# Windowed attention and an ELU feed-forward on one core: first q and k blocks on SyncE, small first tiles, stores on ScalarE

## The chip, the core and the metric

The kernel runs on one core of one Trainium2 chip. The core has five engines that run side by side and meet only at semaphores: TensorE (PE in the profile; its weight loads are listed as PEld), VectorE (DVE), ScalarE (ACT), GpSimd (POOL) and SyncE (SP). SyncE computes nothing here; it asks for transfers. ScalarE and GpSimd can ask for transfers too. Each engine works through its own instructions in the order in which the program gives them, so an instruction that waits holds up everything behind it on its engine. Transfers run on 16 DMA engines; those asked for by GpSimd can change float32 to bfloat16 on the way, those asked for by SyncE or ScalarE cannot.

The metric is the device time of one execution in microseconds, as a median over several runs. The traces are single profiled executions.

## What is computed

```python
# q, k, v: (8, 8, 576, 64) float32; w_in: (512, 2048); w_out: (2048, 512)
scores = (q @ k.transpose(0, 1, 3, 2)) / sqrt(64)
scores = where(abs(pos[:, None] - pos[None, :]) <= 32, scores, -1e9)
attn = softmax(scores)                                # over keys
x = (attn @ v).transpose(0, 2, 1, 3).reshape(4608, 512)
h = x @ w_in
g = where(h > 0, h, exp(min(h, 0)) - 1)
out = g @ w_out                                       # (4608, 512) float32
```

## The kernel before, in words

**Units, groups, tiles.** A unit is 64 query rows of one batch for all 8 heads; nine units make a batch, 72 make the problem. Attention runs over groups of two units (`G`, lines 333 to 337; 37 entries, some of one unit). The feed-forward runs over tiles of units, `sizes = [4, 5, 4, 3] + [8] * 7` (line 494), so that a full tile has 512 token columns.

**One group of attention.** `QK` (line 345) multiplies transposed keys by transposed queries, `SM` (line 355) takes the exponential on ScalarE, `MK` (line 368) multiplies by the window mask on VectorE, `AV` (line 380) multiplies by the values, with a column of ones that gives the sum, `RN` (lines 394 and 396) divides on VectorE, and `X` turns the result for the feed-forward: for the first `NC0 = 8` groups by TensorE and a ScalarE copy (lines 412 and 418), after that by a transposing DMA that SyncE asks for (line 408). The turned columns of a tile lie in `xt`, of which there are two buffers.

**One tile of the feed-forward.** For each of 16 slices `fo` of the 2048 columns, `H` (line 436) runs four matmuls into a PSUM bank `psH` (three banks), `EX` (line 445) takes the exponential on ScalarE, `FF` makes min(e - 1, 0) up to sign, on ScalarE (line 455) or on VectorE (line 457) as `fact` says, and `GG` (lines 463 and 466) takes the maximum on VectorE into `g_sb`. `pack` joins two slices where a tile has four units. `Y` (line 481) multiplies a chunk of 128 tokens by `w_out`, 16 matmuls; `YC` (line 487) copies the bank on ScalarE; `OUT` (line 491) stores 256 KB to DRAM, asked for by SyncE.

**Inputs.** The weights go by eight GpSimd requests that cast (`WI` line 514, `WO` line 519). q and k of batches 0 and 1 go by GpSimd requests too (`LR`, line 307), half a batch per tensor in two requests; TensorE turns them in small transposes (`TR`, line 319), and `ER` copies them out. Those of batch 0 lie in parts of `g_sb` meanwhile, those of batch 1 in the third buffers of `vw` and `qT`. All v blocks, and q and k of batches 2 to 7, are loaded as float32 by SyncE (`L`, line 241) into `st` buffers (14); GpSimd casts them (line 256; batch 0 on VectorE and ScalarE), and for q and k SyncE then asks for a transposing DMA (`XB`, line 273). `GT` (line 249) writes one element of an `st` buffer, so that the load behind it starts no earlier.

**What sets the order.** `Plan` holds every operation with engine, duration, rank, what it depends on, and what it takes and gives back. `Plan.run` plays them through in a small model of engines and DMA rings, on each engine the ready one of lowest rank first, and then issues them in that order. The model's durations, its counts of `st`, `cb`, `psH` and of ring places so decide the written order on each engine's queue; on the chip that order is fixed and only the semaphores decide when each starts. GpSimd's requests have a list of their own (`LINE`, line 579), with at most eight open at a time ("swq").

```python
    LINE = [("0kA",), ("0qA",), ("id",), ("mask",), ("WI", 0), ("WI", 1),
            ("0kB",), ("0qB",), ("WI", 2), ("WI", 3), ("WO", 0), ("WO", 1),
            ("WO", 2), ("1kA",), ("1qA",), ("WO", 3), ("1kB",), ("1qB",)]
```

A transposing DMA of q or k of batch 2 also waits until every `TR` of batch 1 is done, since those read from the buffers that it writes (lines 635 to 640).

Of the kernel before, what the change touches and what calls it, by code (L numbers as in the profile page):

```python
# [20 lines left out]
class Plan:  # L21
# [29 lines left out]
    def run(self):  # L51
# [40 lines left out]
        while len(order) < len(ops) or events or any(rings.values()):  # L92
            heads = [q[0] for q in rings.values() if q]
            per = len(heads)
# [49 lines left out]
            if dma is not None:  # L144
                ring, pk, ns = dma
                heapq.heappush(events, (now + self.QLAT[ring], 2, (
                    ring, [n, pk * ns / 1000.0])))
# [12 lines left out]
def kernel(  # L160
# [33 lines left out]
    NTA = 3  # L194
    NC0 = 8
    NST = 14
# [10 lines left out]
    xtp = ctx.enter_context(tc.tile_pool(name="xtp", bufs=2))  # L207
# [22 lines left out]
    def rows(nm, j):  # L230
        if nm != "v":
            return 128 * j, min(128, S - 128 * j), 0
# [3 lines left out]
    def L(b, nm, j, eng):  # L236
        lo, n, r = rows(nm, j)
# [13 lines left out]

    def copy(eng, dst, src):
# [5 lines left out]
    def C(b, nm, j, eng):  # L258
        _, n, _ = rows(nm, j)
# [5 lines left out]
    def dstT(b, nm, j):  # L265
        _, n, _ = rows(nm, j)
# [4 lines left out]
    def XB(b, nm, j):  # L271
        _, n, _ = rows(nm, j)
        nc.sync.dma_start_transpose(dstT(b, nm, j), live.pop(("C", b, nm, j))[0:n])

# [153 lines left out]
    def pack(t):  # L428
        return 2 if tiles[t][1] == 4 else 1
# [18 lines left out]
    def fact(t, fo):  # L448
        return fo // pack(t) % 2 == 1 if t < NTA else True
# [40 lines left out]
    def OUT(c):  # L490
        nc.sync.dma_start(out[c * 128:c * 128 + 128, :], ys.pop(c))

    NCH = N_TOK // 128
    sizes = [4, 5, 4, 3] + [8] * 7
    tiles, where, tof = [], {}, {}
    p0 = 0
    for t, n in enumerate(sizes):
        for u in range(p0, p0 + n):
            tof[u] = t
            if u == G[gof[u]][0]:  # L500
# [6 lines left out]
              "cb": NCB, "swq": 8, "ring": 2.5})  # L507
# [17 lines left out]
    PER = 4.0  # L525
    LEAD = 36.0
# [47 lines left out]
    def group_of(b, nm, j):  # L574
        if nm == "q":
# [3 lines left out]
    LINE = [("0kA",), ("0qA",), ("id",), ("mask",), ("WI", 0), ("WI", 1),  # L579
            ("0kB",), ("0qB",), ("WI", 2), ("WI", 3), ("WO", 0), ("WO", 1),  # L580
            ("WO", 2), ("1kA",), ("1qA",), ("WO", 3), ("1kB",), ("1qB",)]
    rk = -2000.0
    for x in LINE:
        rk += 1
        if x[0] in ("WI", "WO"):
            fn = {"WI": WI, "WO": WO}[x[0]]
            P.op(x, "POOL", 0.75, rk, [], lambda fn=fn, c=x[1]: fn(c),
                 dma=("P", 32, 104), acq=("swq", 1), rel=("swq", 1))
# [4 lines left out]
        else:  # L593
            b, nm, half = int(x[0][0]), x[0][1], "AB".index(x[0][2])
            for two in range(2):
                P.op(("LR", b, nm, half, two), "POOL", 0.6, rk + 0.1 * two, [],
                     lambda b=b, nm=nm, half=half, two=two: LR(b, nm, half, two),
                     dma=("P", 12, 80), acq=("swq", 1), rel=("swq", 1))
    PK = {"q": [64] * 4 + [32], "k": [64] * 4 + [32], "v": [48] + [64] * 3 + [48]}
    for b in range(B):  # L600
        blocks = sorted(((group_of(b, nm, j), "kqv".index(nm), nm, j)
                         for nm in "kqv" for j in range(NTB)))
        for _, _, nm, j in blocks:
            if b < NBR and nm != "v":
# [3 lines left out]
            eng, ring = "SP", "S"  # L608
            deps = [[], [("GT", b, nm, j)], [("LR", 1, "k", 1, 0)]][min(b, 2)]
            if b == 1:  # L610
                P.op(("GT", b, nm, j), "DVE", 0.1, r - 60, [("WO", 0)],
                     lambda b=b, nm=nm, j=j: GT(b, nm, j))
            P.op(n, eng, 0.4, r - (30 if b > 1 else 60 if b else 1000), deps,
                 lambda b=b, nm=nm, j=j, eng=eng: L(b, nm, j, engs[eng]),
                 dma=(ring, PK[nm][j], 18 if b < 2 else 19), acq=[("st", 1), ("ring", 1)])
            if nm == "v":
                for part in range(3):
# [6 lines left out]
                    if b == 0:  # L624
                        eng = "ACT" if j == 2 or part == 2 and j > 2 else "DVE"
                    P.op(("CV", b, j, part), eng, {"DVE": 0.45, "POOL": 0.7, "ACT": 0.6}[eng],
                         r - 8 + 0.1 * part, deps,
# [3 lines left out]
            P.op(("C", b, nm, j), "POOL", 0.72, r - 8, [n],  # L631
                 lambda b=b, nm=nm, j=j: C(b, nm, j, nc.gpsimd),
                 acq=("cb", 1), rel=("st", 1))
            war = [("QK", last(b - NKB))] if b >= NKB else []
# [3 lines left out]
            P.op(("TT", b, nm, j), "SP", 1.2, r - 6, [("C", b, nm, j)] + war,  # L638
                 lambda b=b, nm=nm, j=j: XB(b, nm, j),
                 dma=("S", 32, 19), acq=("ring", 0.5), rel=("cb", 1))  # L640
    for b in range(NBR):
        for half in range(2):
            r = prank(gof[b * NQB + 4 * half])
            for nm in "kq":
                for part in range(2):
# [6 lines left out]
                    P.op(("TTR", b, nm, half, part), eng, 0.75, r - 4,  # L652
# [152 lines left out]
```

## Time and profile before

| | |
|---|---|
| median of 13 runs | 347.31 us (344.74 to 350.44) |
| the profiled execution | 348.27 us, of it the span from first to last instruction 346.0 us |
| mean granted TensorE clock | 0.98 |
| read from and written to DRAM | 36.70 MB, 9.44 MB |
| requests on SyncE's queue | 100 loads, 60 transposes of q and k, 29 of x, 36 stores |

A profiled span is divided into the busy time of each engine. Requests for transfers are listed apart, as SPq, POOLq and ACTq, with the time for which the engine was held by them; that is not the time of the transfer. In a view of windows each row is one stretch of the span: its length, the busy time of each engine with its number of instructions, the granted TensorE clock, the DMA share (summed over queues, so that it can pass 1) and the bytes moved per time. In a timeline each row has start, duration, engine, line, operation and, in brackets, how long the engine was idle before and what ended that. In a view of one line the durations are least, median and most in nanoseconds, followed by the first and last start.

### The profile page before, as it was taken

How to read it: one execution, taken by the hardware profiler on the slowest of the kernel's cores; microseconds unless marked ns; L12 is line 12 of the kernel's file. 1: busy time of each engine (PE TensorE's matmuls, PEld its weight loads, DVE VectorE, ACT ScalarE, POOL GpSimd, SP SyncE). 2: the span in 40 equal slices, each digit the busy share in tenths (PEclk: the TensorE clock that was granted, in tenths of full speed). 3: DMA queues.
4: the chain of work that ended last, by engine and by line, in shares of the span. 5: the costliest groups of instructions: out<-in, count | busy, mean ns of one | idle time of the engine just before them, and what ended most of it. 6: DMA issues, size and time to landing. Idle time of an engine off the chain costs nothing.

```text
span 346.0 us, 7586 instructions
## 1 busy us (share of the span) xinstructions
PE 308.0 (89%) x2848; PEld 165.0 (48%) x2848; DVE 190.0 (55%) x434; ACT 233.8 (68%) x400; POOL 116.0 (34%) x193
## 2 busy tenths in 40 slices
PE   1598889989989978996999989985999999999995
PEld 1476556666654434442445444432454454444442
DVE  7447878885466576663266646551555655443400
ACT  1748675856778776985478768762778788777711
POOL 8341195755245455344425442436100000000000
PEclk9999999999999999999799999996999999999999
DMA  9999994999998989899899879999431111210021
GB/s 162 204 206 205 205 173 81 231 159 203 206 196 154 234 161 181 152 232 153 189 171 217 182 170 157 209 167 229 86 99 47 45 47 45 68 40 30 33 91 61
DMA packets 151620, 50.89 MB, mean 147 GB/s; under 512 B 139808, under 2 KB 146976, under 8 KB 151584
## 3 DMA queue, kind: packets, MB, share of 16 engines
q1 hardware_dynamic: 144032, 43.86, 66.3%
q0 software_dynamic: 7552, 6.56, 12.0%
q8 instruction: 22, 0.36, 0.4%
q14 instruction: 14, 0.11, 0.1%
HBM read 36.70 MB, written 9.44 MB: 133 GB/s over the span
## 4 chain that ended last, share of the span: by engine, by line
PE 62%; DMA 23%; POOL 3%; DVE 3%; SPq 3%; ACT 3%; issue 2%; POOLq 0%; DVEq 0%; ACTq 0%
PE psH L436 27%; PE psY L481 15%; PE psT L481 11%; DMA qT<-cb 8%; DMA vw<-in_q_dram 4%; DMA xt<-xs 4%; PE psO L380 3%; DMA w_in_sb<-in_moe_w_in_dram 3%; PE psS L345 2%; DMA kT<-cb 2%; SPq L241 2%; DMA st<-in_k_dram 1%; ACT pu L355 1%; DMA st<-in_v_dram 1%; PE psS L481 1%
## 5 line engine op out<-in xcount | busy, mean ns | idle before, releaser
L436 PE MATMUL psH<-xt,w_in_sb 128*128 128x512 bf16 (+3 forms) x704 | 154.3, 349 | 13.1 <-DMA xt<-xs 10.3
L445 ACT ACTIVATE e<-psH 128x512 f32<-128x512 f32 (+2 forms) x160 | 88.3, 555 | 69.9 <-PE psH L436 67.4
L463 DVE SCALAR_TENSOR_TENSOR g_sb<-f,psH 128x512 bf16<-128x512 bf16 (+2 forms) x144 | 91.0, 635 | 50.9 <-ACT f L455 50.4
L436 PEld LDWEIGHTS <-w_in_sb 128*128 128x128 bf16 x704 | 65.3, 100 | 67.0 <-issue 14.3
L455 ACT ACTIVATE f<-e 128x512 bf16<-128x512 f32 (+2 forms) x144 | 85.3, 594 | 3.7
L481 PE MATMUL psY<-w_out_sb,g_sb 128*128 128x512 bf16 x320 | 82.8, 383 | 0.0
L481 PEld LDWEIGHTS <-g_sb 128*128 128x128 bf16 x576 | 53.9, 98 | 58.7 <-issue 2.6
L256 POOL CAST vw<-st 64x512 bf16<-64x512 f32 (+3 forms) x98 | 61.9, 632 | 51.3 <-DMA st<-in_v_dram 45.1
L256 POOL CAST cb<-st 128x512 bf16<-128x512 f32 (+1 forms) x60 | 37.3, 624 | 61.5 <-DMA kT<-cb 33.3
L481 PE MATMUL psT<-w_out_sb,g_sb 128*128 128x512 bf16 x224 | 57.1, 379 | 0.0
L368 DVE TENSOR_TENSOR pm<-pu,masks 128x512 bf16<-128x512 bf16 x72 | 33.5, 505 | 38.3 <-ACT pu L355 38.2
L355 ACT ACTIVATE pu<-psS 128x1024 bf16<-128x1024 f32 (+1 forms) x37 | 37.0, 1000 | 7.8 <-PE psS L345 7.7
L380 PEld LDWEIGHTS <-pm 128*128 128x128 bf16 x576 | 27.5, 100 | 16.6 <-DVE pm L368 2.0
L394 DVE RECIPROCAL rc<-psO 128x4 f32<-128x4 f32 (+1 forms) x71 | 12.8, 180 | 37.5 <-PE psO L380 36.9
L380 PE MATMUL psO<-vw,pm 128*128 128x65 bf16 x552 | 30.1, 196 | 1.9 <-DVE xs L396 0.9
L396 DVE TENSOR_TENSOR xs<-psO,rc 128x256 bf16<-128x256 f32 (+1 forms) x71 | 30.1, 424 | 2.5
L345 PE MATMUL psS<-qT,kT 64*128 64x64 bf16 x576 | 16.2, 193 | 8.2 <-DMA qT<-cb 6.0
L345 PEld LDWEIGHTS <-kT 64*128 64x128 bf16 x576 | 11.7, 96 | 20.8 <-issue 20.4
L319 PE MATMUL psH<-ident,g_sb 48*64 48x48 bf16 x192 | 6.1, 225 | 9.0 <-DMA g_sb<-in_k_dram 7.6
L487 ACT COPY y<-psY 128x512 f32<-128x512 f32 x20 | 11.5, 574 | 3.2 <-PE psY L481 2.9
L319 PEld LDWEIGHTS <-g_sb 48*64 48x64 bf16 x192 | 5.5, 151 | 9.5 <-DMA g_sb<-in_k_dram 7.7
L487 ACT COPY y<-psT 128x512 f32<-128x512 f32 x14 | 8.0, 571 | 2.9 <-PE psT L481 2.9
(48 smaller groups left out, 88.6 us busy)
## 6 DMA issues: line engine op xcount, KB each, us to landing
out_dram<-y SPq DMA_DIRECT2D x36, 256.0 KB, 2.6
st<-in_v_dram SPq DMA_DIRECT2D x24, 256.0 KB, 3.9
st<-in_k_dram SPq DMA_DIRECT2D x24, 256.0 KB, 4.0
st<-in_q_dram SPq DMA_DIRECT2D x24, 256.0 KB, 4.1
st<-in_v_dram SPq DMA_DIRECT2D x16, 192.0 KB, 3.8
w_in_sb<-in_moe_w_in_dram POOLq DMA_DIRECT2D x4, 512.0 KB, 11.8
w_out_sb<-in_moe_w_out_dram POOLq DMA_DIRECT2D x4, 512.0 KB, 13.5
st<-in_k_dram SPq DMA_DIRECT2D x6, 128.0 KB, 3.3
```

What stands on the lines that cost most here:

```text
L256: eng.tensor_copy(dst, src)
L345: nc.tensor.matmul(psS[:, h % 2, s, hp, :], lhsT=kT[b % NKB][base:base + 64, hp, qb * QB:qb * QB + 128], rhs=qT[b % NKB][base:base + 64, h ...
L355: nc.scalar.activation(pu[:, :, 0:n], live.pop(("S", i))[:, :, 0:n], AX.Exp, scale=SCALE)
L368: nc.vector.tensor_mul(dst, pu[:, :, s], mb)
L380: nc.tensor.matmul(o[:, j, :], lhsT=p[:, h, s * QB:s * QB + 128], rhs=vw[b % NVB][:, qb, h, :], start=(s == 0), stop=(s == len(G[i]) - 1))
L396: nc.vector.tensor_mul(live["X", i][0:n, g * HP:(g + 1) * HP, :], o[0:n, :, 0:D], rb)
L436: nc.tensor.matmul(ps[:, f], lhsT=w_in_sb[:, do, (fo + f) * 128:(fo + f + 1) * 128], rhs=xts[t][:, do, :], start=(do == 0), stop=(do == ND ...
L445: nc.scalar.activation(e, ps, AX.Exp)
L455: nc.scalar.activation(f, e, AX.Relu, bias=1.0, scale=-1.0)
L463: nc.vector.scalar_tensor_tensor(g_sb[:, fo:fo + pack(t), gcols(t)], f, -1.0, ps, ALU.mult, ALU.max)
L481: nc.tensor.matmul(ps, lhsT=g_sb[:, fo, gc:gc + 128], rhs=w_out_sb[:, fo, :], start=(fo == 0), stop=(fo == NFO - 1))
L487: nc.scalar.copy(y, ys.pop(c))
```

## The change

The first half of q and k of batch 0 no longer comes by GpSimd's casting requests. SyncE loads it as float32 blocks of 128, 128 and 32 rows (`rows`), first in its queue and mixed with the v blocks (`FIRST`); VectorE casts the k blocks, ScalarE the q blocks, TensorE turns each in four transposes into a `psH` bank (`T`), and ScalarE (k) or VectorE (q) copies it out (`E`). GpSimd makes the identity and the masks first, and then runs a copy of one element (`WAIT`) that reads the landed block `v 0`; all its requests come behind that.

The feed-forward tiles become `[2, 2, 2, 3, 4, 3] + [8] * 7`, with four, two and two slices joined in tiles of 2, 3 and 4 units. `xt` has three buffers instead of two, `st` 12 instead of 14. Nine groups instead of eight are turned by TensorE. In tiles 0 to 4 `FF` alternates between ScalarE and VectorE as it did in tiles 0 to 2; in the tiles of eight units every fourth `FF` goes to VectorE where all were on ScalarE. Stores are asked for by ScalarE, behind the copy `YC`. For batches 2 to 7 the ranks of loads, casts and transposes are 36, 18 and 14 ahead where they were 30, 8 and 6. `H` operations of the first six tiles are no longer tied to one another in order, and the model's durations, ring places and sharing between rings are changed, all of which can alter the written order.

```diff
-    NTA = 3
-    NC0 = 8
-    NST = 14
+    NTA = 5
+    NC0 = 9
+    NXT = 3
+    NST = 12
...
-    xtp = ctx.enter_context(tc.tile_pool(name="xtp", bufs=2))
+    xtp = ctx.enter_context(tc.tile_pool(name="xtp", bufs=NXT))
...
+    spot = const.tile([128, 1], FP32)
+
+    def WAIT(b, nm, j):
+        nc.gpsimd.tensor_copy(spot[64:65], live["L", b, nm, j][64:65, 0:1])
...
+    def T(b, nm, j, bank):
+        _, n, _ = rows(b, nm, j)
+        cb = live.pop(("C", b, nm, j))
+        pool = {"psH": psH_p, "psT": psT_p}[bank]
+        pt = pool.tile([128, HP, 128], BF16, name=bank, tag=bank)
+        for hp in range(HP):
+            nc.tensor.transpose(pt[:, hp, 0:n], cb[0:n, hp * 128:hp * 128 + 128],
+                                ident[0:n, 0:n])
+        live["T", b, nm, j] = pt
+
+    def E(b, nm, j, eng):
+        _, n, _ = rows(b, nm, j)
+        copy(eng, dstT(b, nm, j), live.pop(("T", b, nm, j))[:, :, 0:n])
...
-        return 2 if tiles[t][1] == 4 else 1
+        return {2: 4, 3: 2, 4: 2}.get(tiles[t][1], 1)
...
-        return fo // pack(t) % 2 == 1 if t < NTA else True
+        return fo // pack(t) % 2 == 1 if t < NTA else fo % 4 != 1
...
-        nc.sync.dma_start(out[c * 128:c * 128 + 128, :], ys.pop(c))
+        nc.scalar.dma_start(out[c * 128:c * 128 + 128, :], ys.pop(c))
...
-    sizes = [4, 5, 4, 3] + [8] * 7
+    sizes = [2, 2, 2, 3, 4, 3] + [8] * 7
...
-              "cb": NCB, "swq": 8, "ring": 2.5})
+              "cb": NCB, "swq": 8, "ring": 3.2})
...
+    LL, CC, XX = 36, 18, 14
...
-    LINE = [("0kA",), ("0qA",), ("id",), ("mask",), ("WI", 0), ("WI", 1),
-            ("0kB",), ("0qB",), ("WI", 2), ("WI", 3), ("WO", 0), ("WO", 1),
+    FIRST = [("k", 0), ("k", 1), ("q", 0), ("v", 0), ("v", 1), ("q", 1),
+             ("k", 2), ("v", 2), ("q", 2), ("v", 3), ("v", 4)]
+    LINE = [("id",), ("mask",), ("wait",), ("WI", 0), ("WI", 1), ("0kB",), ("0qB",),
+            ("WI", 2), ("WI", 3), ("WO", 0), ("WO", 1),
             ("WO", 2), ("1kA",), ("1qA",), ("WO", 3), ("1kB",), ("1qB",)]
...
+    GATE = ("v", 0)
...
+            P.op(x, "POOL", 0.1, rk, [("L", 0) + GATE], lambda: WAIT(0, *GATE))
...
-                 dma=("P", 32, 104), acq=("swq", 1), rel=("swq", 1))
+                 dma=("P", 32, 81), acq=("swq", 1), rel=("swq", 1))
...
-            P.op(n, eng, 0.4, r - (30 if b > 1 else 60 if b else 1000), deps,
+            rl = r - (LL if b > 1 else 60) if b else -1999 + FIRST.index((nm, j))
...
-            P.op(("TT", b, nm, j), "SP", 1.2, r - 6, [("C", b, nm, j)] + war,
+            P.op(("TT", b, nm, j), "SP", 1.3, r - XX, [("C", b, nm, j)] + war,
...
-        if t >= 2:
-            deps.append(("H", t - 2, NFO - pack(t - 2)))
+        if t >= NXT:
+            deps += [("H", t - NXT, fo) for fo in range(0, NFO, pack(t - NXT))]
...
-        if n:
+        if n and t >= 6:
             deps.append(("H",) + hseq[n - 1])
...
-        if n >= 3:
-            deps.append(("FF",) + hseq[n - 3])
...
-        P.op(("OUT", c), "SP", 0.4, r, [("YC", c)],
-             lambda c=c: OUT(c), dma=("S", 8, 90))
+        P.op(("OUT", c), "ACT", 0.42, r, [("YC", c)],
+             lambda c=c: OUT(c), dma=("A", 8, 90))
```

More of the change, by code (lines that the diff above doesn't have):

```diff
@@ L641 @@
     for b in range(NBR):
-        for half in range(2):
+        for half in range(0 if b else 1, 2):
             r = prank(gof[b * NQB + 4 * half])
@@ L742 @@
         deps = [("FF", t, fo)]
[L743 to L745 removed]
+        if u0 < NQB and fo + pack(t) > 12:
+            deps += [("TR", 0, nm, 1, part) for nm in "kq" for part in range(2)]
+        P.op(("GG", t, fo), "DVE", 0.12 + 0.52 * fr, r, deps,
              lambda t=t, fo=fo: GG(t, fo), rel=("psH", 1))
```

105 lines of the change are left out of this document (64 added, 41 removed).

## The prediction, made before the changed kernel was run

> **What bounds the kernel now.** I began with the page (engine shares, and the chain that ended last), then took windows by stage.
>
> ```profile
> PE 308.0 (89%) x2848; PEld 165.0 (48%) x2848; DVE 190.0 (55%) x434; ACT 233.8 (68%) x400; POOL 116.0 (34%) x193
> PE 62%; DMA 23%; POOL 3%; DVE 3%; SPq 3%; ACT 3%; issue 2%; POOLq 0%; DVEq 0%; ACTq 0%
> ```
>
> ```profile
> 0.00:20.00 20.00, 8.13 (x184) 6.61 (x186) 12.51 (x37) 8.30 (x11) 12.99 (x28) 1.00 1.14 185
> 20.00:40.00 20.00, 17.36 (x256) 13.28 (x251) 13.21 (x38) 13.52 (x24) 3.32 (x6) 1.00 1.25 206
> 56.00:250.00 194.00, 175.83 (x1537) 92.25 (x1532) 111.58 (x255) 136.18 (x237) 86.27 (x139) 0.96 1.01 184
> 250.00:346.00 96.00, 92.00 (x593) 43.09 (x591) 39.78 (x79) 64.50 (x106) 0.00 (x0) 1.00 0.17 55
> 185.00:190.00 5.00, 5.00 (x46) 2.38 (x45) 2.79 (x5) 4.16 (x7) 4.23 (x7) 1.00 1.35 237
> 235.00:240.00 5.00, 2.54 (x14) 1.17 (x15) 0.18 (x1) 0.60 (x2) 2.64 (x5) 0.50 1.14 201
> ```
>
> TensorE is idle for 38 us of 346: 11.9 in the first 20, 18.2 between 56 and 250, 4.0 at the very end, little elsewhere. From 250 on it has 92.0 us of work in 96: nothing there can be won by waiting less. In the middle it is also throttled after each long wait (0.50 at 235 to 240), which at a mean clock of 0.96 is another 0.04 x 194 = 7.8 us. So 26 us at most lie in the middle, and something feeds TensorE too slowly there. The chain says DMA, so I looked at the queue that asks for them, SyncE's, around the last long wait:
>
> ```profile
> 228.53 1.22 SPq L273 DMA_TRANSPOSE kT<-cb  x1
> 229.80 0.58 SPq L241 DMA_DIRECT2D st<-in_v_dram  x1
> 230.43 0.57 SPq L241 DMA_DIRECT2D st<-in_k_dram  x1
> 231.10 1.32 SPq L273 DMA_TRANSPOSE qT<-cb  x1
> 232.53 0.53 SPq L491 DMA_DIRECT2D out_dram<-y  x1
> 233.10 0.42 SPq L241 DMA_DIRECT2D st<-in_q_dram  x1
> 233.62 1.34 SPq L408 DMA_TRANSPOSE xt<-xs  x1
> 237.46 1.86 PE L436 MATMUL psH<-xt,w_in_sb 128*128 128x512 bf16 x4 [5.35 <-DMA xt<-xs]
> ```
>
> Each request starts some 0.05 to 0.1 us after the one ahead: SyncE never rests, and the x transpose on which TensorE waited 5.35 us stood in line behind a q transpose, a store and a load. The rows of its four lines from 56 to 250 say whether that holds throughout:
>
> ```profile
> L273 SPq DMA_TRANSPOSE kT<-cb x30: 1195/1250/3094, 56.6 to 247.5; - x30
> L273 SPq DMA_TRANSPOSE qT<-cb x29: 1192/1222/3564, 63.2 to 246.2; - x29
> L408 SPq DMA_TRANSPOSE xt<-xs x22: 1188/1214/1805, 71.6 to 242.3; - x22
> L491 SPq DMA_DIRECT2D out_dram<-y x21: 367/525/1633, 55.7 to 248.8; - x21
> L241 SPq DMA_DIRECT2D st<-in_v_dram x29: 425/578/1507, 56.1 to 238.3; - x29
> L241 SPq DMA_DIRECT2D st<-in_q_dram x29: 379/581/1603, 59.5 to 237.7; - x29
> L241 SPq DMA_DIRECT2D st<-in_k_dram x28: 383/580/727, 58.9 to 235.6; - x28
> ```
>
> By medians: 59 transposes of q and k 72.9 us, 22 of x 26.7, 86 loads 49.9, 21 stores 11.0; together 160.5. With 188 gaps of about 0.08 (15) that is 175.5 of 194, and the maxima, two to three times the medians, account for the rest. **SyncE's time to ask is the bound from 56 to 250 us**, TensorE's from there on.
>
> **The change part by part.** *Stores to ScalarE.* Taken off SyncE: 21 x (0.525 + 0.08) = 12.7. But a load behind a store takes 0.42 instead of 0.58 (rows 233.10 and 229.80), which is lost for most of them: 18 x 0.16 = 2.9. Net 9.8 us. The bytes still pass the same DMA engines, whose share is 1.01 over the stretch; but 237 GB/s against the mean of 184 have been moved in one window, so there is room. SyncE's long requests (up to 3.56) show that it is sometimes held up. Asking 6% faster I charge 2 us more of that; bounds 0 and 9.8, all of the gain.
>
> The Trainium skill, "DMA: Bandwidth & Descriptors", section "Issuing engines are not separate DMA queues", says that spreading requests over engines saves only the time that the sequencer needs to ask, usually small against the transfer. The trace agrees on what is saved, but here that time is what runs out; by the rule's word "small" this term would be near 0 and the sum below near 3.
>
> *On ScalarE* a store costs what it cost on SyncE, 0.525 (bounds 0.367 and 1.633), and 36 of them 18.9 us. It is paid for:
>
> ```profile
> L455 ACT ACTIVATE f<-e 128x512 bf16<-128x512 f32 x120 | 75.8, 633 | 3.0
> L457 DVE TENSOR_SCALAR f<-e 128x512 bf16<-128x512 f32 x8 | 3.4, 428 | 4.3 <-ACT e L445 4.3
> ```
>
> Four of 16 `FF` in seven tiles go to VectorE: 28 x 0.633 = 17.7 us off ScalarE, 28 x 0.428 = 12.0 onto VectorE. ScalarE is busy 136 of the 194 us, VectorE 112; so neither becomes the bound on average, and I set both at 0. Behind the store on ScalarE stand `EX` and `SM`, for which TensorE waits through its three `psH` banks; that is a rival below. After the last matmul copy and store follow one another as before: 0.
>
> *One more group turned by TensorE* (`NC0` 9): 1.214 + 0.08 = 1.3 us off SyncE; the four transposes on TensorE and a copy cost under 1 us at 70 us, where TensorE hardly waits: 0.
>
> *Where SyncE's stretch starts.*
>
> ```profile
> SPq L491 <- ACT y L487: 9.1, 1, 9.1
> 30.71 0.58 POOL L307 DMA_DIRECT2D vw<-in_k_dram  x1 [2.02 <-DMA w_out_sb<-in_moe_w_out_dram]
> 45.46 0.58 POOL L307 DMA_DIRECT2D qT<-in_q_dram  x1
> 55.18 0.94 PE L319 MATMUL psH<-ident,qT 48*64 48x48 bf16 x48
> 56.61 2.19 SPq L273 DMA_TRANSPOSE kT<-cb  x1
> ```
>
> From 46.5 to 55.66 SyncE is held by the first store, whose data isn't ready. Without it the next load goes out at once, but the first k transpose of batch 2 must also wait for the last `TR` of batch 1 (55.18 + 0.94 = 56.1): alone worth 0.5 us. That `TR` is late because its request, due some 2 us behind that of 30.71, stands at 45.46 behind v casts on GpSimd. The model's cheaper requests may put it ahead of them; if so, up to 8 us. I take 2, near the lower end, since GpSimd's requests also start later (next).
>
> *The start.*
>
> ```profile
> 5.95 1.54 POOL L514 DMA_DIRECT2D w_in_sb<-in_moe_w_in_dram  x2
> 13.30 0.70 PE L345 MATMUL psS<-qT,kT 64*128 64x64 bf16 x16 [1.10 <-DVE qT L256]
> 14.25 0.74 POOL L519 DMA_DIRECT2D w_out_sb<-in_moe_w_out_dram  x1 [2.46 <-DMA w_in_sb<-in_moe_w_in_dram]
> 22.80 3.52 PE L436 MATMUL psH<-xt,w_in_sb 128*128 128x256 bf16 x16
> L241 SPq DMA_DIRECT2D st<-in_v_dram x5: 401/574/1661, 0.8 to 3.8; - x5
> 5.05 3.27 DVE L256 CAST vw<-st 32x512 bf16<-32x512 f32 x6
> L256 POOL CAST cb<-st 64x512 bf16<-64x512 f32 x12 | 7.3, 609 | 13.5 <-DMA kT<-cb 13.1
> 0.31 0.10 POOL L789 MEMSET const-float32-0.0<- 128x1 f32 x1 [0.31 <-issue]
> DMA to landing us min/median/max: 8.0/11.8/14.2
> ```
>
> Removed: four requests, 96 small transposes, four copies. Added: six loads (6 x 0.574 = 3.4 us on an otherwise free SyncE), six casts, 24 transposes, six copies. A first block of 192 KB, sharing with GpSimd's requests, is cast at 5.05; k 0, k 1 and q 0 are 768 KB, so at the 0.2 MB/us of the first window the third is there at about 8, and cast, turning and copy, each taken at the 0.6 of a cast, give the first `QK` at about 9.7 instead of 13.3. `v 0` is fourth, at about 9; the one-element copy is priced between a 0.10 us memset and a 0.61 us cast, 0.2, nearer to the one-column memset. So w_in is asked for at about 9.2 instead of 5.95, without the four requests ahead of it. Its first chunk was there at 14.2 (the request at 14.25 needed its place); now 9.2 plus 8.0, the shortest landing of a w_in chunk (last row), is 17. Behind the waiting copy stand all 20 requests of GpSimd, so batch 1's blocks come up to 3 us later, too, less what the four removed ones took. For TensorE: the first `H` at 17 to 18 rather than 22.8, since a two-unit tile needs only group 0, but the later w_in chunks 2 to 3 later. TensorE may be 2 us ahead at 40, or 2 behind. As SyncE's stretch sets what follows, 0 of it reaches the end (bounds 4 gained, 3 lost).
>
> *Three `xt` buffers, longer leads, freer order.* They change which request comes first, not how many; as SyncE's stretch has no free time they can't shorten it: 0, up to 5 if the line is better sorted.
>
> *The clock.* From the chain:
>
> ```profile
> 297.10 0.86 PE psH L436 x4
> ```
>
> Four matmuls take 0.86 us there and took 1.86 behind the wait at 237.46. With shorter waits some of this goes: I take 2 us of the 7.8 (bounds 0 and 7.8).
>
> **Sum:** 9.8 + 1.3 + 2 (start of the stretch) + 2 (clock) - 2 (held up) = 13.1 us; 348.27 - 13.1 = 335.2 against the profiled execution. That execution lies 0.96 above the median of the runs, so **334 us**.
>
> **The rivals.**
>
> *All waits of the middle go* (the stretch starts 8 us earlier, its line is better sorted): 13.1 + 6 + 5 = 24, near the 26 of the middle: about 323. For it: the hold of 9.1 us. Against: the last `TR`.
>
> *The two engines that ask hinder each other.* While ScalarE generates a store, SyncE's request waits as long as the store takes, so the 9.8 comes back and so does the 2 for being held up: about 342. No trace here has two such queues at work, so nothing in it speaks against. The Trainium skill, "Perfetto Trace Analysis", section "DMA Instruction — HWDGE (DVE, Sync)", states that the block generating descriptors is shared by the sequencers and locked for one request at a time; no run here shows it yet.
>
> *The DMA engines are the bound:* share 1.01. Then 9.8 and 1.3 bring nothing: 334 + 11.1 - 2 = 343, and 347 if start and clock bring nothing either. Against it: 237 GB/s at 185.
>
> *ScalarE's stores stop TensorE (the slower side).* The store waits in ScalarE's line for its copy, then holds it 0.4 to 1.6 us; meanwhile no `EX` empties a `psH` bank, and `SM` of the next group is late. With three banks and `Y` between, TensorE can go on for some 3 x 0.86 us. If each of 36 stores costs TensorE more than 13.1 / 36 = 0.36 us, the gain is gone; at 0.5 it is 18 us and the time 352. For it: the longest store on SyncE held it 1.633 us, and at 1.2 us and more two such delays use up the banks. Against: ScalarE's idle time, 58 of 194 us.
>
> *It doesn't do what it says:* the planner's new order puts other waits where the stores stood: 346.
>
> **How the numbers follow.** The forecast (327 to 341) 0.55; all waits go (318 to 327) 0.12; hindered asking (341 to 345.5) 0.10; DMA bound 0.09, half of it faster by over 0.5%; ScalarE stops TensorE 0.10, nearly all of it slower; other waits 0.04, half of it no change. Faster by over 0.5% (the least that a measurement of this kernel tells from none): 0.83; within it 0.06; slower 0.11. The range runs from 322 to 346, leaving out some 0.04 below and 0.14 above.
>
> **What would show it.** After: 28 rather than 29 x transposes and no store on SPq; SyncE's stretch ending at about 237 instead of 250, still without rests; TensorE's idle time in it down from 18 to about 8, and its clock above 0.96; stores on ACTq at about 0.5 us, with ACT no busier than before. First `QK` near 9.7, first `H` near 17.5. If store and transpose times both grow, the hindering rival holds; if transposes grow with a DMA share well above 1.01, the DMA bound; if TensorE waits for `EX`, the slower one. Rests on SyncE's queue would mean that I mistook the bound.

## The result: 339.65 us, and the profile after

| | before | after |
|---|---|---|
| median of runs | 347.33 us (48 runs, 344.4 to 350.94) | 339.65 us (11 runs, 335.74 to 343.4) |
| ratio, 95% interval | | 0.9758 [0.9724, 0.9792] |
| profiled execution, its span | 348.27, 346.0 us | 338.0, 335.6 us |

The ratios here and below compare only the faster of a kernel's runs, since some of its runs are one or two per cent slower whatever the edit; the traces of two experiments, the stores back on SyncE and the old tiles, were taken in such slower runs.

The kernel became 2.4% faster. The forecast was 334, with 322 to 346 as its range: the direction is right, the time lies within the range, and the gain is smaller than forecast. The forecast took 13.3 us off the median; 7.7 came, or 10.3 between the two profiled executions.

The page of the changed kernel, engine shares and the chain that ended last:

```profile
PE 303.8 (91%) x2908; PEld 167.0 (50%) x2908; DVE 199.4 (59%) x451; ACT 215.1 (64%) x357; POOL 114.5 (34%) x190
PE 75%; DMA 9%; DVE 7%; ACT 5%; SPq 2%; issue 2%; ACTq 0%; DVEq 0%
```

The chain now goes through TensorE for 75% of the span where it was 62, and through transfers for 9% where it was 23. TensorE's account gives the 10.4 us by which the span shrank: it is idle for 335.6 - 303.8 = 31.8 us instead of 38.0, and busy for 4.2 us less. The windows of the changed kernel, cut like those of before, say where (length; busy us of PE, PEld, DVE, ACT, POOL; granted clock, DMA share, GB/s):

```profile
0.00:20.00 20.00, 6.62 (x88) 5.31 (x89) 10.33 (x33) 9.85 (x16) 8.26 (x22) 1.00 1.00 187
20.00:40.00 20.00, 18.44 (x400) 16.36 (x399) 15.34 (x45) 15.08 (x27) 6.99 (x11) 1.00 1.25 203
56.00:246.00 190.00, 177.36 (x1577) 93.87 (x1574) 120.84 (x267) 127.13 (x213) 89.24 (x143) 0.99 0.89 186
246.00:335.60 89.60, 85.93 (x541) 40.11 (x536) 40.59 (x82) 53.23 (x88) 0.00 (x0) 1.00 0.16 53
```

In the middle TensorE is idle 12.6 us instead of 18.2, and the clock there rose from 0.96 to 0.99: by the prediction's own count the throttle cost 7.8 us there and now costs 0.01 x 190 = 1.9. That window flatters the change, because one throttled stretch now lies ahead of it. Two windows of the changed kernel:

```profile
42.00:47.00 5.00, 5.00 (x70) 3.90 (x70) 2.42 (x6) 3.39 (x5) 1.30 (x3) 0.66 1.19 208
192.00:200.00 8.00, 5.12 (x45) 2.53 (x46) 2.33 (x5) 2.94 (x5) 3.81 (x7) 1.00 0.75 169
```

In the first the clock is 0.66, although TensorE is busy throughout; in the second it is 1.00, although the longest wait of the middle lies there (3.49 us, up to 194.88). The first 20 us hold 1.5 us less TensorE work than before, the next 20 us 1.1 more.

SyncE's rows of the changed kernel from 59 us to 246 us, and the stores on ScalarE's queue over the whole span (least, median, most in ns; first and last start):

```profile
L280 SPq DMA_TRANSPOSE kT<-cb x30: 1188/1272/2930, 59.5 to 241.6; - x30
L280 SPq DMA_TRANSPOSE qT<-cb x30: 1192/1216/2418, 62.6 to 244.1; - x30
L429 SPq DMA_TRANSPOSE xt<-xs x22: 1190/1222/2387, 70.2 to 242.8; - x22
L242 SPq DMA_DIRECT2D st<-in_v_dram x27: 573/782/1516, 58.5 to 235.6; - x27
L242 SPq DMA_DIRECT2D st<-in_q_dram x27: 384/608/1615, 65.5 to 233.6; - x27
L242 SPq DMA_DIRECT2D st<-in_k_dram x26: 379/580/1083, 64.7 to 232.9; - x26
L512 ACTq DMA_DIRECT2D out_dram<-y x36: 338/338/399, 52.4 to 332.6; - x36
```

The stores are gone from SyncE and take 0.338 us each on ScalarE, where 0.525 was set. But the last transpose of q or k ends at 244.1 + 1.2 = 245.3, where it ended at 251.7 before and 237 was forecast for the end of the stretch, and the loads of v now hold SyncE for 0.782 us at the median instead of 0.578.

The last long wait of TensorE is again for an x transpose. SyncE's request and the matmul behind it in the changed kernel's timeline:

```profile
225.52 1.22 SPq L429 DMA_TRANSPOSE xt<-xs  x1
228.06 1.02 PE L457 MATMUL psH<-xt,w_in_sb 128*128 128x512 bf16 x4 [2.54 <-DMA xt<-xs]
```

It ends at 228.06 instead of 237.46, 9.4 us earlier, and was 2.54 us instead of 5.35. From there to the end it is 335.6 - 228.06 = 107.5 us, and was 346.0 - 237.46 = 108.5. So nearly the whole gain was made before this point, in the stretch that SyncE feeds. And it is SyncE's queue that made TensorE wait there. The last halves of the two `xs` tiles that these x transposes turn, before and after:

```profile
225.64 0.42 DVE L396 TENSOR_TENSOR xs<-psO,rc 128x256 bf16<-128x256 f32 x1
219.91 0.42 DVE L417 TENSOR_TENSOR xs<-psO,rc 128x256 bf16<-128x256 f32 x1
```

Before, the data was ready at 226.06 and asked for at 233.62, 7.6 us later; after, it was ready at 220.33 and asked for at 225.52, 5.2 us later.

### The profile page after: what moved, and what is told of

It is laid out like the page before. It is cut to its first block, busy times and chain, and to the rows that moved or that the text cites. A ratio compares the mean times of both kernels' runs of the same rounds, so it can differ in the third digit from the quotient of the medians.

```text
span 335.6 us, 7663 instructions
## 1 busy us (share of the span) xinstructions
PE 303.8 (91%) x2908; PEld 167.0 (50%) x2908; DVE 199.4 (59%) x451; ACT 215.1 (64%) x357; POOL 114.5 (34%) x190
## 4 chain that ended last, share of the span: by engine, by line
PE 75%; DMA 9%; DVE 7%; ACT 5%; SPq 2%; issue 2%; ACTq 0%; DVEq 0%
PE psH L457 33%; PE psY L502 18%; PE psT L502 13%; PE psO L401 4%; DMA xt<-xs 4%; DMA st<-in_v_dram 4%; PE psS L366 3%; SPq L242 2%; ACT e L466 2%; DMA qT<-cb 2%; DVE g_sb L484 1%; DVE g_sb L487 1%; ACT pu L376 1%; DVE pm L389 1%; PE psS L502 1%
## 5 line engine op out<-in xcount | busy, mean ns | idle before, releaser
L457 PE MATMUL psH<-xt,w_in_sb 128*128 128x512 bf16 (+3 forms) x832 | 151.3, 320 | 17.5 <-DMA xt<-xs 11.2
L466 ACT ACTIVATE e<-psH 128x512 f32<-128x512 f32 (+1 forms) x148 | 86.5, 586 | 85.8 <-PE psH L457 69.8
L457 PEld LDWEIGHTS <-w_in_sb 128*128 128x128 bf16 x832 | 70.7, 100 | 65.5 <-issue 17.8
L484 DVE SCALAR_TENSOR_TENSOR g_sb<-f,psH 128x512 bf16<-128x512 bf16 (+1 forms) x106 | 70.7, 667 | 34.2 <-ACT f L476 33.0
L476 ACT ACTIVATE f<-e 128x512 bf16<-128x512 f32 (+1 forms) x106 | 65.8, 620 | 2.5
L415 DVE RECIPROCAL rc<-psO 128x4 f32<-128x4 f32 (+1 forms) x71 | 12.7, 180 | 30.8 <-PE psO L401 30.4
L487 DVE TENSOR_TENSOR g_sb<-psH,f 128x512 bf16<-128x512 f32 (+1 forms) x42 | 28.5, 678 | 3.3
L478 DVE TENSOR_SCALAR f<-e 128x512 bf16<-128x512 f32 (+1 forms) x42 | 19.3, 460 | 7.0 <-ACT e L466 6.7
L366 PEld LDWEIGHTS <-kT 64*128 64x128 bf16 x576 | 11.1, 97 | 13.5 <-issue 11.6
## 6 DMA issues: line engine op xcount, KB each, us to landing
w_out_sb<-in_moe_w_out_dram POOLq DMA_DIRECT2D x4, 512.0 KB, 14.9
```

Of the source, the lines that this page charges most:

```text
L366: nc.tensor.matmul(psS[:, h % 2, s, hp, :], lhsT=kT[b % NKB][base:base + 64, hp, qb * QB:qb * QB + 128], rhs=qT[b % NKB][base:base + 64, h ...
L457: nc.tensor.matmul(ps[:, f], lhsT=w_in_sb[:, do, (fo + f) * 128:(fo + f + 1) * 128], rhs=xts[t][:, do, :], start=(do == 0), stop=(do == ND ...
L466: nc.scalar.activation(e, ps, AX.Exp)
L476: nc.scalar.activation(f, e, AX.Relu, bias=1.0, scale=-1.0)
L484: nc.vector.scalar_tensor_tensor(g_sb[:, fo:fo + pack(t), gcols(t)], f, -1.0, ps, ALU.mult, ALU.max)
L487: nc.vector.tensor_tensor(g_sb[:, fo:fo + pack(t), gcols(t)], ps, f, ALU.max)
```

## The experiments

The theory to be tested, A in the expectations, is the prediction's own: SyncE's time to ask is the bound, and the stores taken off it are the gain. The other letters stand for rivals, by which the stores bring little and the time is set elsewhere: by a later start of SyncE's stretch, or by other requests that grow once the stores are gone, because transfers or casts hold them. All ratios are against the kernel before on the same chip; the changed kernel stands at 0.9758. Each edit changes the planner's order too wherever it changes a duration or a rank.

### The stores, in the changed kernel and alone

The first puts the stores back on SyncE in the changed kernel; the second is the kernel before with nothing but its stores moved.

```diff
-        nc.scalar.dma_start(out[c * 128:c * 128 + 128, :], ys.pop(c))
+        nc.sync.dma_start(out[c * 128:c * 128 + 128, :], ys.pop(c))
...
-        P.op(("OUT", c), "ACT", 0.42, r, [("YC", c)],
-             lambda c=c: OUT(c), dma=("A", 8, 90))
+        P.op(("OUT", c), "SP", 0.4, r, [("YC", c)],
+             lambda c=c: OUT(c), dma=("S", 8, 90))
```

> The changed kernel with one thing undone: SyncE asks for the stores again, the rest stays. Theory A (the gain is SyncE's line: 21 stores of 0.63 us off its stretch, whose start the busy DMA engines set): 339.65 + 10 = about 349, SyncE's stretch again some 194 us long. Theory B (the gain is TensorE's, from the early first q and k and the small tiles): 340 to 341. Theory C (the DMA engines bound the middle whoever asks): 340 to 342.

> The kernel before with one thing of the change: ScalarE asks for the stores. Theory A: 347.33 - 9 = about 338, as fast as the whole change or faster. Theories B and C: 346 to 348, no gain. The rival that ScalarE's stores stop TensorE, here without the FF operations that the change moves to VectorE: above 347.

Back on SyncE: 346.28 us, 0.9944 [0.989, 0.9998]. Within the change the stores are worth 0.9944 / 0.9758, that is 1.9%, and without them little of its gain is left; B and C (340 to 342) missed. Alone: 344.51 us, 0.9921 [0.9884, 0.9957], only 0.8%, where A wanted 338 and B and C wanted none. The trace of the second kernel shows why A missed, in the rows of SyncE's transposes, of the stores and of the window from 60 to 240:

```profile
L273 SPq DMA_TRANSPOSE kT<-cb x30: 1188/1300/3777, 53.2 to 244.1; - x30
L273 SPq DMA_TRANSPOSE qT<-cb x30: 1172/1382/2733, 60.5 to 245.7; - x30
L491 ACTq DMA_DIRECT2D out_dram<-y x36: 338/338/412, 55.6 to 339.0; - x36
```

```profile
60.00:240.00 180.00, 162.11 (x1411) 85.89 (x1436) 103.75 (x236) 126.90 (x224) 82.54 (x133) 0.98 1.07 187
```

With the stores gone the transposes grew: by medians 30 x (1.300 - 1.250) + 30 x (1.382 - 1.222) = 6.3 us, half of the 12.7 that had been taken off. Added up row by row, with the loads, it is more: between the first and the last transpose of q and k the stores gave 12.9 us back, and the other requests took 11.5 us more. So the other requests do grow once the stores are gone, in a kernel where nothing else was changed. SyncE's stretch is no shorter, 194.5 us where it was 195.1; it only starts earlier, at 53.2 instead of 56.6.

### The element that `GT` writes

```diff
-            if b == 1 or (b, nm, j) == (2, "k", 0):
...
+            if b == 1:
...
-                deps = [("GT", 2, "k", 0)]
+                deps = [("LR", 1, "k", 1, 0)]
```

> The changed kernel without the one-element write on VectorE that stands ahead of the loads of batch 2 (the planner keeps the order without it, as the kernel before did). It came at 46.12 us, and the last v load of batch 1 held SyncE until 47.52. Theory A, with the DMA engines holding SyncE there: 339.65 within 1. Rival, that this wait on VectorE is what starts SyncE's stretch 5.5 us later than before: 335 to 336, the first load of batch 2 near 42.

338.26 us, 0.9736 [0.9683, 0.9788]: the same as the changed kernel. The first load of batch 2 isn't held by that write in a way that matters: without it that load went out at 48.46, with it at 47.62, and not near 42. The first transpose of batch 2 then came at 61.5 instead of 59.5, and the kernel took no longer; where the stretch starts doesn't alone set the time.

### The old start

GpSimd's casting requests bring all of q and k of batch 0 again and nothing waits for `v 0`; tiles, stores and leads stay as changed.

```diff
-            return 128 * j, min(128, (S if b else S // 2) - 128 * j), 0
+            return 128 * j, min(128, S - 128 * j), 0
...
-    LINE = [("id",), ("mask",), ("wait",), ("WI", 0), ("WI", 1), ("0kB",), ("0qB",),
+    LINE = [("0kA",), ("0qA",), ("id",), ("mask",), ("WI", 0), ("WI", 1), ("0kB",), ("0qB",),
...
-            if b == 1 and nm != "v" or b == 0 and (nm, j) not in FIRST:
+            if b < NBR and nm != "v":
...
```

> The changed kernel with the old start: the first half of q and k of batch 0 by GpSimd's casting requests again, ahead of w_in, no wait on v 0; stores, tiles, leads as changed. Theory A: the stretch of SyncE starts near 42 again instead of 47.6, so 334 to 336. Theory B: what the early first QK won is lost, 343 to 346. No difference (339 to 341) if what the start wins on TensorE and loses on the DMA engines cancel.

335.94 us, 0.9635 [0.9543, 0.9727], about 1.2% faster than the changed kernel; the intervals just touch. The run further below that has the old start and no `GT` write gave the same ratio with a narrower interval, [0.9581, 0.969]. So the new start costs time. The number is the one that A named, but not for A's reason: the first load of batch 2 went out at 46.21, not near 42. In the changed kernel's timeline the start reads:

```profile
7.26 0.34 POOL L257 COPY spot<-st 1x1 f32<-1x1 f32 x1 [4.67 <-DMA st<-in_v_dram]
7.82 1.65 POOL L535 DMA_DIRECT2D w_in_sb<-in_moe_w_in_dram  x2 [0.21 <-issue]
8.51 0.61 PE L366 MATMUL psS<-qT,kT 64*128 64x64 bf16 x16 [0.71 <-DVE qT L263]
17.71 0.62 ACT L261 CAST vw<-st 64x512 bf16<-64x512 f32 x1 [4.92 <-DMA st<-in_v_dram]
18.23 0.57 ACT L439 COPY xt<-psT 128x512 bf16<-128x512 bf16 x1
18.86 1.87 PE L457 MATMUL psH<-xt,w_in_sb 128*128 128x128 bf16 x16 [5.03 <-ACT xt L439]
```

The first `QK` runs at 8.51 instead of 13.30 and the first `H` at 18.86 instead of 22.80, as meant. `H` waits for its `xt` copy, and that stands on ScalarE behind the cast of a v block which came late. What is lost lies on SyncE. Its requests for the v blocks of batch 1, and what follows, in the changed kernel:

```profile
32.37 15.14 SPq L242 DMA_DIRECT2D st<-in_v_dram  x5
47.62 1.92 SPq L242 DMA_DIRECT2D st<-in_k_dram  x2
59.47 2.96 SPq L280 DMA_TRANSPOSE kT<-cb  x2
```

in the kernel before:

```profile
32.80 9.28 SPq L241 DMA_DIRECT2D st<-in_v_dram  x5
42.12 1.88 SPq L241 DMA_DIRECT2D st<-in_k_dram  x2
```

and with the old start in the changed kernel:

```profile
32.24 12.03 SPq L242 DMA_DIRECT2D st<-in_v_dram  x5
46.21 0.99 SPq L242 DMA_DIRECT2D st<-in_k_dram  x2
L280 SPq DMA_TRANSPOSE kT<-cb x30: 1193/1248/2885, 58.0 to 239.8; - x30
```

The same five requests hold SyncE for 9.28, 12.03 and 15.14 us. What holds them longer wasn't separated. One thing that differs is GpSimd's casting transfers, which begin behind the wait (7.82 instead of 5.95). Their queue (packets, MB, share of 16 engines) between 20 and 60 us in the changed kernel,

```profile
q0 software_dynamic: 5182, 4.57, 70.5%
```

and in the kernel before:

```profile
q0 software_dynamic: 4554, 4.04, 63.4%
```

With the old start their share there is 61.1%, smaller than before the change, and the five requests still take 12.03 us instead of 9.28. So this share alone doesn't explain the hold.

The first transpose of batch 2 goes out at 59.47, with the old start at 58.0, before at 56.61. From the changed kernel to the one with the old start that is 1.5 us of some 4; the old start also puts 2.5 us more TensorE work into the first 20 us (9.08 us there, against 6.62). The rest stays open.

### Leads and small tiles

The leads of the kernel before (30, 8 and 6) in the changed kernel; then, the other way, the kernel before with its stores moved and the new leads; then the changed kernel with the old tiles.

```diff
-    LL, CC, XX = 36, 18, 14
+    LL, CC, XX = 30, 8, 6
```

> The changed kernel with the old leads (ranks of loads, casts and transposes of batches 2 to 7 ahead by 30, 8 and 6). Theory A (SyncE's asking time bounds the middle): only the sort of the line changes, 339.65 within 2. Rival D (the leads decide: requests no longer hold up SyncE when loads go in a row ahead of the transposes, which is why the stores bring 7 us here and 2.7 in the kernel before): 343 to 345.

The second has the stores' diff above the other way round, and 36, 18 and 14 where the kernel before has 30, 8 and 6.

> The kernel before with two things of the change: ScalarE asks for the stores, and the leads are 36, 18 and 14. The stores alone gave 0.9921, undoing the leads in the changed kernel cost 0.0103. Theory A with the sort of the line: the two together 0.975 to 0.983. Rival, that the stores' gain needs the moved FF, the small tiles or the third x buffer: 0.987 to 0.995.

The third:

```diff
-    NTA = 5
+    NTA = 3
...
-        return {2: 4, 3: 2, 4: 2}.get(tiles[t][1], 1)
+        return 2 if tiles[t][1] == 4 else 1
...
-    sizes = [2, 2, 2, 3, 4, 3] + [8] * 7
+    sizes = [4, 5, 4, 3] + [8] * 7
...
-        if n and t >= 6:
+        if n and t >= 4:
```

> The changed kernel with the old first tiles, 4, 5, 4 and 3 units. Theory A: SyncE's stretch is the same, so 0.974 to 0.979 as with the small tiles. Theory B (small tiles bring TensorE's gain at the start): 0.985 or more.

Old leads: 343.69 us, 0.9861 [0.9757, 0.9964], so the new leads are worth about 1%, though the intervals touch; A (within 2 of 339.65) missed, and the time is the one that rival D named. In the kernel before, stores and leads together give 344.8 us, 0.983 [0.9765, 0.9895], against 0.9921 for the stores alone; these intervals overlap as well. Both point the same way, neither is sharp. Old tiles: 347.56 us, 0.9944 [0.989, 0.9998]: here A missed and B's 0.985 or more came. The small tiles, priced at nothing, are worth 1.9% beside the new start. In the trace with the old tiles SyncE's stretch is about as long (188 us, against 186), but it starts 2.9 us later, and TensorE has 22.2 us of work in the first 40, against 25.1. So part of the loss is made ahead of the stretch; from 60 to 240 TensorE then idles 19.7 us, against 12.6. What delays the start wasn't followed up, and with the old start the tiles weren't tried.

### Fewer requests on SyncE, and more

If asking is the bound, taking another kind of request off SyncE must gain. Here ScalarE asks for the 30 k loads of batches 2 to 7:

```diff
-            P.op(n, "SP", 0.6 if b else 0.4, rl, deps,
-                 lambda b=b, nm=nm, j=j: L(b, nm, j, nc.sync),
-                 dma=("S", pk, 18 if b else 15), acq=[("st", 1), ("ring", 1)])
+            le, lq = ("ACT", "A") if b > 1 and nm == "k" else ("SP", "S")
+            P.op(n, le, (0.45 if le == "ACT" else 0.6) if b else 0.4, rl, deps,
+                 lambda b=b, nm=nm, j=j, le=le: L(b, nm, j, engs[le]),
+                 dma=(lq, pk, 18 if b else 15), acq=[("st", 1), ("ring", 1)])
```

> The changed kernel with the 30 k loads of batches 2 to 7 asked for by ScalarE too, same bytes and packets. It takes 30 x 0.66 = 20 us off SyncE. Theory A (SyncE's asking time is the bound): most waits of TensorE in the middle go, 331 to 335. Theory C (the DMA engines' work is the bound, SyncE is only held up by them): 338 to 341, the other requests on SyncE longer instead. If ScalarE is held up by the loads: slower than 341.

336.01 us, 0.9624 [0.9532, 0.9716], 1.3% below the changed kernel. The direction is A's; by the ratio the time would be 334, within A's 331 to 335. SyncE's q transposes and the window in this kernel:

```profile
L280 SPq DMA_TRANSPOSE qT<-cb x30: 1188/1354/2796, 63.2 to 221.7; - x30
```

```profile
60.00:240.00 180.00, 169.44 (x1482) 90.71 (x1508) 117.08 (x257) 121.13 (x204) 85.37 (x137) 0.97 0.98 190
```

SyncE is done 22.4 us earlier (221.7 against 244.1), but the time falls by only about 4.6 us. TensorE still idles 10.6 of these 180 us, against 12.6, and is throttled to 0.97, so A's "most waits go" didn't happen. Its long waits there are two, both for x transposes again, of 3.4 and 3.67 us. The second:

```profile
220.42 1.24 SPq L280 DMA_TRANSPOSE kT<-cb  x1
221.75 1.20 SPq L280 DMA_TRANSPOSE qT<-cb  x1
223.04 1.25 SPq L429 DMA_TRANSPOSE xt<-xs  x1
226.12 1.46 PE L457 MATMUL psH<-xt,w_in_sb 128*128 128x512 bf16 x3 [3.67 <-DMA xt<-xs]
```

Its data was ready at 217.25; the request went out 5.8 us later, behind the last four transposes of q and k, two of which are shown. So there it is still the order in SyncE's queue. In the first the request went out 1.2 us after its data and landed 4.5 us after that.

The opposite test separates asking from moving. Each load of batches 2 to 7 becomes two requests of half the columns, read as they lie in DRAM in rows of 1 KB. It loads other elements than the attention needs, the same number of bytes to the same buffers, so only its time is to be read.

```diff
+        if b < 2:
...
+        else:
+            flat = SRC[nm][b].rearrange("h s d -> (h s d)").rearrange("(x c) -> x c", c=H * D)
+            for c0 in (0, 256):
+                eng.dma_start(out=t[r:r + n, c0:c0 + 256],
+                              in_=flat[lo:lo + n, c0:c0 + 256])
```

> The changed kernel with each load of batches 2 to 7 replaced by two requests of half the columns that read rows of 1 KB as they lie in DRAM (the same bytes, other elements of q, k and v): a quarter of the packets, twice the requests. SyncE's time for a load should be about the same (2 x 0.34 = 0.68 against 0.66, by the stores of 2 KB rows that took 0.338). Theory A: 339 to 342. Theory C: the DMA engines' work is smaller, 328 to 334, requests on SyncE no longer held up, DMA share well below 0.9.

358.91 us, 1.0274 [1.0177, 1.0371], some 5% slower than the changed kernel. Both theories missed: C wanted a gain, and A wanted no change, because it took two halves at 0.68 us together. They take 0.95. SyncE's rows and the window:

```profile
L249 SPq DMA_DIRECT2D st<-in_q_dram x54: 334/430/1575, 67.0 to 254.6; - x54
L249 SPq DMA_DIRECT2D st<-in_v_dram x52: 377/431/1681, 59.7 to 248.6; - x52
L249 SPq DMA_DIRECT2D st<-in_k_dram x52: 342/570/1712, 65.7 to 253.3; - x52
L286 SPq DMA_TRANSPOSE qT<-cb x30: 1182/1205/2194, 64.5 to 265.5; - x30
```

```profile
60.00:240.00 180.00, 156.41 (x1346) 82.02 (x1367) 103.07 (x231) 105.26 (x182) 79.10 (x125) 0.96 0.66 169
```

For comparison, the same window of the changed kernel:

```profile
60.00:240.00 180.00, 167.36 (x1472) 87.94 (x1469) 114.33 (x253) 119.56 (x200) 85.57 (x137) 0.99 0.90 188
```

The DMA engines have less to do, a share of 0.66 instead of 0.90, and the kernel is slower: they aren't the bound. SyncE asks for 158 loads in 75.3 us by medians where it asked for 80 in 52.6, and its stretch ends at 266.7, 21 us later. Added up row by row the loads took 27.5 us more, the gaps 5.8 more and the transposes 13.2 less; that makes the stretch 20 us longer, and the kernel lost some 18.

### `FF` on ScalarE

```diff
-        return fo // pack(t) % 2 == 1 if t < NTA else fo % 4 != 1
+        return fo // pack(t) % 2 == 1 if t < NTA else True
```

> The changed kernel with all FF of the eight-unit tiles on ScalarE as before: 17.7 us more on ScalarE, 12 less on VectorE. Theory A: neither engine bounds, 339.65 within 2. Rival (ScalarE's stores need the room that the moved FF make, which is why the stores alone bring only 2.7 us in the kernel before): 343 to 346.

337.35 us, 0.9658 [0.9491, 0.9826]: no loss is seen, though the interval is wide. The rival is refuted; moving a quarter of `FF` to VectorE isn't needed, and ScalarE, with the stores and all of `FF`, doesn't stop TensorE.

### Putting the better parts together

The edits are those shown above, joined: the old start without the `GT` write, and the same with the k loads on ScalarE.

> The changed kernel with the old start (as in the run before, 0.9635 of the kernel before) and without the one-element write ahead of the loads of batch 2. With the old start the last v load of batch 1 left SyncE at 44.27 and the loads waited until 46.21. Theory A: the stretch starts up to 1.9 us earlier, ratio 0.958 to 0.964. Rival, that the queues are full there anyway: 0.9635, no change.

> The same with the k loads of batches 2 to 7 asked for by ScalarE. Moving them brought 0.9758 to 0.9624 with the new start. If both gains add: 0.945 to 0.952. If ScalarE's line, now holding 66 requests, or the DMA engines (share 1.1 in that run) take over: 0.958 to 0.966.

The old start without the `GT` write gives 335.27 us, 0.9635 [0.9581, 0.969], the same as the old start alone, as the rival said. With the k loads on ScalarE as well it is 334.2 us, 0.9546 [0.9457, 0.9635]: the fastest of all, 4.5% below the kernel before and 2.2% below the change. Whether the two gains add in full, the interval doesn't tell.

## Why the prediction came out as it did

**The bound** was placed rightly, in SyncE's queue. With stores back the gain goes, with twice as many load requests the time rises although the DMA engines are less busy, with 30 fewer it falls. "SyncE never rests" was right as well: in the kernel before, the gaps between the first and the last transpose of q and k are 14.9 of 195.1 us, and only three of 186 are longer than 0.15 us. Nor do the rows hide waits for data. The kernel before shows this at its first store, whose data came late:

```profile
45.36 1.13 SPq L241 DMA_DIRECT2D st<-in_v_dram  x1
55.66 0.37 SPq L491 DMA_DIRECT2D out_dram<-y  x1
```

SyncE stood at this store from 46.5 on, and the row is still only 0.37 us long. What was wrong is to give each kind of request a fixed price. Six requests in a row in the changed kernel, and a cast by GpSimd:

```profile
210.61 0.57 SPq L242 DMA_DIRECT2D st<-in_k_dram  x1
211.24 0.68 SPq L242 DMA_DIRECT2D st<-in_q_dram  x1
211.96 1.14 SPq L242 DMA_DIRECT2D st<-in_v_dram  x1
213.20 2.93 SPq L280 DMA_TRANSPOSE kT<-cb  x1
216.23 1.21 SPq L280 DMA_TRANSPOSE qT<-cb  x1
217.53 1.22 SPq L429 DMA_TRANSPOSE xt<-xs  x1
199.48 0.61 POOL L263 CAST cb<-st 64x512 bf16<-64x512 f32 x1 [1.81 <-DMA st<-in_k_dram]
```

The k transpose at 213.20 is the sixth from the last, so it turns the last block of batch 6, the one of 64 rows. Its cast, the last row, had ended at 200.09, 13 us earlier; the 2.93 us aren't a wait for it. The request stands behind three loads. In the changed kernel's stretch the first load of a run takes 0.58 us at the median, the second 0.61, the third 0.74, the fourth 0.96; a transpose behind another transpose takes 1.22, behind three loads 1.58, behind four 1.84. The v blocks are mostly third. Where loads have a quarter of the packets (the split loads), transposes behind them stay at 1.20 to 1.22. With the stores alone moved, transposes behind two loads went from 1.31 to 1.65. So the price points to transfers that are still under way; how the packets hold SyncE up, no run shows.

**The stores** are a term that was mis-sized, with the step "Asking 6% faster I charge 2 us more of that". Gross 12.7 us stands. The prediction gave back 2.9 for the loads behind stores and 2 for being held up, 4.9 together. The stretch from the first transpose of q or k to the end of the last, added up row by row:

| | requests | SyncE held | from, to | length |
|---|---|---|---|---|
| before | 187 | 180.2 us | 56.6 to 251.7 | 195.1 us |
| stores alone | 167 | 178.8 | 53.2 to 247.7 | 194.5 |
| changed | 161 | 172.9 | 59.5 to 245.3 | 185.9 |
| changed, stores back | 180 | 182.7 | 62.0 to 259.2 | 197.2 |
| changed, k loads on ScalarE | 132 | 146.7 | 59.5 to 223.0 | 163.4 |
| changed, split loads | 240 | 187.2 | 60.7 to 266.7 | 206.0 |

From before to changed, 20 stores of 12.9 us are gone and six loads of 3.6, which now go ahead of the first transpose; held time fell by only 7.3. So the rest took 9.2 us more, 7.2 of it in the loads. With the stores alone it was 11.5. That is about twice the 4.9 of the prediction. That the stretch became 9.2 us shorter, as the prediction's 9.8 + 1.3 - 2 = 9.1 had it, is luck: the six loads made up for what the price took.

**One more x group** on TensorE: 28 instead of 29 transposes, as said; but 22 of them lie in the stretch in both traces, so its 1.3 us doesn't show there. It wasn't tried alone.

**The start of the stretch** was set at 2 us earlier and came 2.9 us later (59.47 against 56.61); this is the other term that missed. The reason given for it holds by itself: with only the stores moved it came 3.4 us earlier (53.2). The rest of the change put it back by more, of which the old start explains 1.5 us. The stretch so ends 6.4 us earlier instead of the 11.1 that these terms give. **The start** itself was set at 0 and costs about 1.2%, some 4 us, by the old start's run, a little past the bound of 3 lost. The point forecasts within it came near: first `QK` 8.51 (9.7 forecast), first `H` 18.86 (17.5), though not for the reason given: a v cast on ScalarE was last, not w_in.

**The clock** gave more than the 2 us set, but not the 5.9 that the middle window suggests. Before, the windows from 160 to 170 and from 234 to 242 have 0.66 and 0.57, that is 3.4 us lost in each; after, 42 to 47 and 97 to 101 have 0.66 and 0.57, 1.7 us each. So 6.8 us became 3.4, and some of the 6.8 fell on time in which TensorE waited anyway. "Throttled after each long wait" doesn't hold in the changed kernel, by the two windows shown with the result. **Leads and small tiles** were set at 0 (up to 5), with the reason that the line has no free time. About 1% and 1.9% came. The reason fails, since the line's length depends on its order and its start can move; by which of the two the leads gained wasn't shown. These single values don't add up: stores 1.9, tiles 1.9 and leads 1.0, less 1.2 for the start, would be 3.6%, while 2.4% came. The parts aren't independent of one another.

So the forecast 13.1 was a sum in which too much went to the stores and the start of the stretch and too little to tiles, leads and clock. That it ended less than 6 us off is partly luck, these errors meeting.

**The rivals.** *Hindered asking*: a store on ScalarE's queue took 0.338 us beside SyncE's work, never over 0.399, and SyncE's transposes stayed at medians of 1.272 and 1.216 (1.250 and 1.222 before). The 17 of them during which a store was being asked for took 1.218 at the median, the other 65 took 1.223. The lock of the Trainium skill's "Perfetto Trace Analysis", section "DMA Instruction — HWDGE (DVE, Sync)", shows in no row here, which neither confirms nor excludes it. *DMA bound*: the split loads speak against it, with a lower DMA share and a longer time. *ScalarE stops TensorE*: ACT went from 233.8 to 215.1 us busy, and with all of `FF` back no loss appeared. *Other waits where the stores stood* comes nearest to what the stores alone showed, as longer requests and not as waits. *All waits go*: TensorE's idle time in the middle fell to 12.6, not to the 8 of the forecast.

The rule of "DMA: Bandwidth & Descriptors", section "Issuing engines are not separate DMA queues" in the Trainium skill, that a second asking engine saves only the time to ask, usually a small one, fits this case for a single request: a load held SyncE for 0.58 us and landed some 4 us after it was asked for, by the medians of the kernel before. What it leaves out is the sum over one queue: moving 36 stores was worth 1.9% within this kernel, moving 30 loads 1.3% more.

## What to carry to other kernels

Where many small transfers feed the bound engine, add up the queue that asks for them, by median and count, beside the DMA share: a queue without rests can be the bound while the transfers themselves aren't, and moving requests to an engine with idle time can pay. But don't take a request's price as fixed. Look at what stands ahead of it in the queue, and add up the rows and not only the medians: with only the stores moved, most of what was taken off came back as longer rows of the rest, above all of transposes right behind loads. Undo the parts of a change one at a time: here one part cost 1.2% within a change that gained 2.4%.

## What was not expected of the hardware

A store of 256 KB held ScalarE's queue for 0.338 us at the median and SyncE's, before, for 0.525. A load split in two held SyncE for two times 0.43 to 0.57 us instead of once 0.58 to 0.78: two halves cost nearly twice the asking, although each has larger rows and half the bytes. And five requests for loads held SyncE for 15.14 us while GpSimd's casting transfers were in progress, two of them for 0.33 and 0.49 us and three for 3.8 to 5.5, where a load in the middle takes 0.6 to 0.8: asking has no fixed price. In the middle, too, the third load of a run took 0.74 us at the median where the first took 0.58.
